# A convolution and ELU feed-forward kernel: four 64x64 array tiles for both matmuls, and the clamp of the exponential on GpSimd

## The chip, the cores and the metric

One core of one Trainium2 chip. Times are microseconds of device time (us). Unless a run says otherwise they are medians of timed runs; several experiments were run once ("one look"), and their state is then called unknown. Engines are named as in the profile: PE is TensorE, PEld its weight loads, DVE VectorE, ACT ScalarE, POOL GpSimd, SP SyncE, which here only issues DMAs.

## The reference

```python
# x (8, 4096, 192) float32, weight (8, 7), w_in (192, 2048), w_out (2048, 192)
w = softmax(weight)                       # per head, over 7 taps
attn[b, s, h*24+g] = sum_k w[h, k] * x[b, s-6+k, h*24+g]     # causal convolution
h = attn.reshape(32768, 192) @ w_in
g = where(h > 0, h, exp(min(h, 0)) - 1)   # ELU
out = g @ w_out                           # (32768, 192) float32
```

Two matmuls of 32768 x 192 x 2048, with an ELU on 32768 x 2048 values between them.

## The kernel before

Tokens go in 64 groups of 512. The convolution of a group is 40 small matmuls in four 32-column tiles of the array. Its 192 channels land in 2 x 128 partitions, 24 used of every 32, and w_in is padded to the same rows, so the first matmul takes two K steps of 128. A free row carries a bias of 1, so PSUM holds h+1.

```python
# PE, one chunk of 128 hidden units x 512 tokens: K = 2 x 128 with padding
pe.matmul(dst, wpadA[:, P*cc:P*(cc+1)], attnT[:, s, 0, :], start=True,  stop=False)
pe.matmul(dst, wpadB[:, P*cc:P*(cc+1)], attnT[:, s, 1, :], start=False, stop=True)
...
# ACT: E = exp((h+1) - 1), a bias tensor of -1
a.activation(E[:, C % NE, :], hps[...], ACT.Exp, bias=negone[:, 0:1], scale=1.0)
...
# DVE: max(min(E, 1), h+1) = ELU + 1, one instruction
v.scalar_tensor_tensor(out=gT[...], in0=E[...], scalar=1.0, in1=hps[...],
                       op0=ALU.min, op1=ALU.max)
...
# DVE: the output, minus the column sums of w_out, which takes the 1 away again
v.tensor_tensor(osb[...], ops_slot[CC % 2], negcs[:], ALU.add)
```

GpSimd only issues the loads of x and of the weights (float32 to narrower types on the way) and sets up constants.

## Time and profile before

| | before |
|---|---|
| time | 884.62 us (884.52 to 884.67) |
| PE, DVE, ACT, POOL busy | 95%, 83%, 80%, 11% of 882.3 us |
| one group of 512 tokens | 13.38 us, so 26.76 us per 1024 tokens |
| first matmul 128x512, start to start | 0.216 us |
| second matmul 128x192, start to start | 82.5 ns |

The first line below is the page's busy times by engine, with the share of the span and the number of instructions. The second is the chain that ended last, by engine: the last instruction followed back, step by step, to what released each one. The others are the page's groups: line, engine, operation, tiles, shapes, count; then busy us and mean ns of one; then the idle time before them and what ended most of it.

```profile
PE 833.8 (95%) x8594; PEld 561.6 (64%) x8722; DVE 730.6 (83%) x1300; ACT 709.1 (80%) x1160; POOL 98.9 (11%) x170
...
PE 80%; DVE 11%; ACT 6%; issue 2%
...
L456 DVE SCALAR_TENSOR_TENSOR gT<-E,hps 128x512 f16<-128x512 f32 x1024 | 652.2, 684 | 139.2 <-ACT E L424 136.7
L424 ACT ACTIVATE E<-hps,negone 128x512 f32<-128x512 f32 x1024 | 641.7, 689 | 121.5 <-PE hps L385 121.5
L340 PE MATMUL ops<-w_outq,gT 128*128 128x192 f16 x4096 | 421.2, 246 | 10.0 <-DVE gT L456 1.0
L385 PE MATMUL hps<-attnT,wpadB 128*128 128x512 bf16 x1022 | 388.1, 380 | 13.2 <-issue 9.8
```

PE is both the busiest engine and most of the chain. A matmul's recorded length overlaps the next one's, so its pace is read from the chain in order of time (start us, us, what): 0.22 for each first matmul, 0.66 for eight second ones.

```profile
403.28 0.22 PE hps L378
403.50 0.22 PE hps L385
...
404.14 0.66 PE ops L340 x8
```

One more line: the output DMAs on SP, with the least, median and greatest ns that one issue holds SP.

```profile
L473 SPq DMA_DIRECT2D out_dram<-osb x8: 332/332/333, 395.9 to 419.5; - x8
```

### The profile page before, as it was taken

To read this page: it belongs to the slowest core of one execution; us is meant where nothing else is said; L and a number is where in the kernel's file an instruction comes from. 1 tells how busy PE (TensorE), PEld (TensorE's weight loads), DVE (VectorE), ACT (ScalarE), POOL (GpSimd) and SP (SyncE) were. 2 spreads that over 40 slices of the span, in tenths; PEclk is the share of its full clock that TensorE was granted. 3 is DMA by queue.
4 is the path that set the end of the run, shared out by engine and by line. 5 is a ranking of instruction groups with operands and counts; after the bars stand their busy time and mean duration, and the time that the engine had idled before them with its cause. 6 is when DMAs were issued, how large, how long until landed. Compare 5 with 4: busy or idle time off the path is not lost.

```text
span 882.3 us, 21974 instructions
## 1 busy us (share of the span) xinstructions
PE 833.8 (95%) x8594; PEld 561.6 (64%) x8722; DVE 730.6 (83%) x1300; ACT 709.1 (80%) x1160; POOL 98.9 (11%) x170
## 2 busy tenths in 40 slices
PE   0899999999999999999999999999999999999998
PEld 0466666666666666666666666666666666666666
DVE  6788888888888888888888888888888888888886
ACT  2888888888888888888888888888888888888884
POOL 6101101001001011011011011011011011011000
DMA  7233233233233233232233232232232232232311
GB/s 93 34 50 55 41 54 55 39 56 50 44 55 51 45 55 51 43 55 49 46 51 53 46 51 50 47 52 47 48 55 46 48 56 45 50 55 41 54 33 42
DMA packets 82586, 43.89 MB, mean 50 GB/s; under 512 B 49523, under 2 KB 82291, under 8 KB 82483
## 3 DMA queue, kind: packets, MB, share of 16 engines
q0 software_dynamic: 45616, 17.30, 18.5%
q1 hardware_dynamic: 36866, 25.18, 9.2%
q8 instruction: 69, 1.13, 0.5%
q14 instruction: 35, 0.28, 0.1%
HBM read 34.57 MB, written 25.17 MB: 68 GB/s over the span
## 4 chain that ended last, share of the span: by engine, by line
PE 80%; DVE 11%; ACT 6%; issue 2%
PE ops L340 35%; PE hps L385 22%; PE hps L378 20%; DVE gT L456 10%; ACT E L424 5%; PE cps L300 4%; DVE Ttmp L267 1%; DVE Tm L270 0%; PE ops L357 0%; ACT L280 0%; DVE Tm L264 0%; ACT attnT L412 0%; ACT wpadB L282 0%; ACT wpadA L281 0%; ACT attnT L413 0%
## 5 line engine op out<-in xcount | busy, mean ns | idle before, releaser
L456 DVE SCALAR_TENSOR_TENSOR gT<-E,hps 128x512 f16<-128x512 f32 x1024 | 652.2, 684 | 139.2 <-ACT E L424 136.7
L424 ACT ACTIVATE E<-hps,negone 128x512 f32<-128x512 f32 x1024 | 641.7, 689 | 121.5 <-PE hps L385 121.5
L340 PEld LDWEIGHTS ops<-w_outq,gT 128*128 128x128 f16 x4096 | 348.2, 98 | 145.0 <-DVE gT L456 40.7
L340 PE MATMUL ops<-w_outq,gT 128*128 128x192 f16 x4096 | 421.2, 246 | 10.0 <-DVE gT L456 1.0
L385 PE MATMUL hps<-attnT,wpadB 128*128 128x512 bf16 x1022 | 388.1, 380 | 13.2 <-issue 9.8
L378 PE MATMUL hps<-attnT,wpadA 128*128 128x512 bf16 x898 | 341.9, 381 | 3.4 <-DVE gT L456 2.0
L378 PEld LDWEIGHTS hps<-attnT,wpadA 128*128 128x128 bf16 x1024 | 100.0, 98 | 82.0 <-DVE gT L456 15.6
L385 PEld LDWEIGHTS hps<-attnT,wpadB 128*128 128x128 bf16 x1024 | 100.4, 98 | 61.0 <-issue 0.8
L198 POOL DMA_DIRECT2D xg<-in_x_dram x64 | 48.1, 752 | 647.2 <-PE cps L300 621.2
L440 DVE TENSOR_TENSOR osb<-ops,negcs 128x192 f32<-128x192 f32 x256 | 89.9, 351 | 4.2 <-PE ops L340 4.2
L412 ACT ACTIVATE attnT<-cps 128x512 bf16<-128x512 f32 x64 | 38.2, 597 | 42.1 <-PE cps L300 42.1
L300 PE MATMUL cps<-Tm,xg 128*24 128x122 bf16 (+1 forms) x2560 | 41.8, 210 | 16.3 <-DVE Tm L270 16.3
L300 PEld LDWEIGHTS cps<-Tm,xg 128*24 128x24 bf16 x2560 | 33.2, 92 | 26.6 <-DVE Tm L270 16.4
L413 ACT ACTIVATE attnT<-cps 128x512 bf16<-128x512 f32 x64 | 37.8, 591 | 0.0
L200 POOL DMA_DIRECT2D xg<-in_x_dram x64 | 34.8, 544 | 0.0
L182 POOL MEMSET xg<- 6x192 bf16 x8 | 2.0, 248 | 82.5 <-PE cps L300 82.5
L267 DVE TENSOR_TENSOR Ttmp<-shift,wprb 128x976 bf16<-128x976 bf16 x6 | 7.1, 1176 | 0.2
L185 POOL DMA_DIRECT2D xg<-in_x_dram x8 | 4.5, 561 | 0.0
L270 DVE TENSOR_TENSOR Tm<-Tm,Ttmp 128x976 bf16<-128x976 bf16 x6 | 4.0, 667 | 0.2
L316 PE MATMUL ops<-wrow,onesF 1*128 1x56 f32 x2 | 0.6, 422 | 3.0 <-POOL onesF L157 3.0
L236 DVE TENSOR_REDUCE wmx<-ops 128x8 f32<-128x56 f32 x1 | 0.2, 217 | 3.7 <-PE ops L316 3.7
L316 PEld LDWEIGHTS ops<-wrow,onesF 1*128 1x128 f32 x2 | 0.5, 308 | 3.0 <-issue 3.0
(31 smaller groups left out, 22.3 us busy)
## 6 DMA issues: line engine op xcount, KB each, us to landing
out_dram<-osb SPq DMA_DIRECT2D x256, 96.0 KB, 1.6
xg<-in_x_dram POOLq DMA_DIRECT2D x56, 192.0 KB, 3.6
xg<-in_x_dram POOLq DMA_DIRECT2D x64, 48.0 KB, 3.6
xg<-in_x_dram POOLq DMA_DIRECT2D x8, 144.0 KB, 3.6
w_outq<-in_moe_w_out_dram POOLq DMA_DIRECT2D x1, 768.0 KB, 9.4
wpadA<-in_moe_w_in_dram POOLq DMA_DIRECT2D x4, 96.0 KB, 3.8
wpadB<-in_moe_w_in_dram POOLq DMA_DIRECT2D x4, 96.0 KB, 4.8
xg<-in_x_dram POOLq DMA_DIRECT2D x8, 45.8 KB, 2.3
```

Source lines behind the costliest of these rows:

```text
L198: g.dma_start(xg[:, s, w0:NWIN_FULL, :], src).then_inc(s_xin[s], 16)
L200: g.dma_start(xg[:, s, 4, :], x_flat[t0 + LASTW_ROW0 : t0 + GS, :]).then_inc(s_xin[s], 16)
L267: v.tensor_tensor(Ttmp[:, :, :], sd, wd, ALU.mult).then_inc(s_dset)
L300: ins = pe.matmul(cps[SLOT * q : SLOT * q + CH_PER_HEAD, col0 + ocol : col0 + ocol + ncol], xg[:, s, wdw, CH_PER_HEAD * hq : CH_PER_HEAD * ...
L340: ins = pe.matmul(bank, gT[:, slot, c, P * j : P * (j + 1)], w_outq[:, c, :], start=(c == 0), stop=(c == NCH - 1),)
L378: pe.matmul(dst, wpadA[:, P * cc : P * (cc + 1)], attnT[:, s, 0, :], start=True, stop=False,)
L385: pe.matmul(dst, wpadB[:, P * cc : P * (cc + 1)], attnT[:, s, 1, :], start=False, stop=True,).then_inc(s_mm1)
L412: a.activation(attnT[:, slot, 0, :], cps[:, 0:GS], ACT.Copy).then_inc(s_attn)
L413: a.activation(attnT[:, slot, 1, :], cps[:, GS : 2 * GS], ACT.Copy).then_inc(s_attn)
L424: a.activation(E[:, C % NE, :], hps[:, (C // 2) % NHTB, (C % 2) * GS : (C % 2) * GS + GS], ACT.Exp, bias=negone[:, 0:1], scale=1.0,).then_ ...
L440: v.tensor_tensor(osb[:, CC % 4, :], ops_slot[CC % 2], negcs[:], ALU.add).then_inc(s_oev)
L456: v.scalar_tensor_tensor(out=gT[:, G % 2, c, :], in0=E[:, C % NE, :], scalar=1.0, in1=hps[:, (C // 2) % NHTB, (C % 2) * GS : (C % 2) * GS ...
```

## The change

The intent is to take work off PE. 192 channels are exactly three K steps of 64, so in 64x64 tiles, four at once, the padding goes. That leaves no bias row, so PSUM holds h itself, and ELU becomes max(min(E, 1) - 1, h): the min and the subtraction go to the idle GpSimd, and VectorE keeps one maximum, over 1024 elements at once. Work goes in 32 supers of 1024 tokens, 16 pairs of hidden blocks each. The output matmuls ("rounds") of a super run three pairs behind the next super's. The convolution still writes 24 channels of every 32 partitions, so 20 SBUF-to-SBUF DMAs per super pack them into 64-row blocks, twice. Pairs and convolutions take turns in three PSUM buffers ("slots"): a slot is free for the next once VectorE, or for a convolution ACT, has read it.

```diff
+HALF_STEPS = (10, 9, 9, 9, 9, 9, 9)     # output rounds per pair
+CONV_AT = (2, 10)                       # pairs after which the next super's convolutions run
...
+                for u in range(2):                       # GpSimd
+                    W(s_exp, 2 * n + u + 1)
+                    g.tensor_scalar(out=E[:, n % NE, u, :], in0=E[:, n % NE, u, :],
+                        scalar1=1.0, scalar2=1.0, op0=ALU.min, op1=ALU.subtract,
+                    ).then_inc(s_clp)
...
-                    a.activation(E[...], hps[...], ACT.Exp, bias=negone[:, 0:1], scale=1.0)
+                        a.activation(E[:, n % NE, u, :], H[:, k, GS*u:GS*(u+1)], ACT.Exp)
...
-                    v.scalar_tensor_tensor(... op0=ALU.min, op1=ALU.max)
-                v.tensor_tensor(osb[...], ops_slot[...], negcs[:], ALU.add)
+                v.tensor_tensor(gT[... 1024], E[... 1024], H[:, slot, :], ALU.max)
...
+                    for j in range(3):                   # PE, first matmul
+                        for r in range(2):
+                            for c in range(2):
+                                pe.matmul(H[HP*c:HP*(c+1), k % 3, GS*r:GS*(r+1)],
+                                    w_in[HP*r:HP*(r+1), j, ...], att[HP*r:HP*(r+1), s % 2, j, c, :],
+                                    start=(j == 0), stop=(j == 2), tile_position=(HP*r, HP*c))
...
+                    for (hb, sl, r0, nr, j, d0) in MOVES:   # SP: 10 moves, two copies each
+                        for r in range(2):
+                            sy.dma_start(att[HP*r+d0 : HP*r+d0+nr, s % 2, j, :, :],
+                                csb[SLOT*sl+r0 : SLOT*sl+r0+nr, s % 2, hb, :, :]).then_inc(s_att, 16)
```

(Shortened, with cuts marked. GpSimd issues the x loads of a later super before its clamp of pair 8.)

## The prediction

> **What bounds the kernel now.** TensorE. In the page's first part PE is busy 95% of 882.3 us, DVE 83%, ACT 80%, POOL 11%; the chain that ended last is 80% PE. In the timeline a 512-token group takes 13.38 us (26.76 per 1024 tokens): 32 first matmuls 0.216 us apart (6.9), 64 second matmuls 82.5 ns apart (5.3), 40 convolution matmuls in 0.6, the rest short waits for exp and DVE. 64 groups are 856 us; head 22, tail about 8.
>
> **What the change removes and adds, per 1024 tokens (estimates from those durations).**
> - First matmul: K is 3x64 instead of 2x128 padded, so 16 pairs x 3 x 0.216 = 10.4 us instead of 13.8, if four 64x64 tiles stream together. The convolution's four column tiles do: 40 matmuls in 0.6 us.
> - Second matmul: same streaming, 128 rounds x 82.5 ns = 10.6 us, but four 64-column weight loads a round. The trace spaces its 24-column loads about 10 ns apart; if loads go one at a time, 64 columns are 27 ns and a round 107 ns, 13.7 us.
> - Convolution and switches about 2 us. PE sum 23 to 26 us.
> - ACT: exp without bias tensor should step by 0.50 us like the copies (0.58 now): 16 + evacuations 3.5 = 19.5.
> - DVE: one 128x1024 maximum, (1024+145)/0.96 = 1.22 us x 16 = 19.5; its 0.35 us output additions go.
> - POOL: 32 clamps. The Trainium skill ("GPSIMD Engine Reference", section 3.1) gives 1.03 cycles an element at 1.2 GHz for short bodies, about 0.55 us for 512; the affine select here ran nearer 1.5 ns an element, 0.85 us. So 18 to 27 us plus about 1.5 us of x issues.
> - PSUM: three slots shared by all; a slot's cycle is 0.8 + 1.1 + 0.65 + 1.25 + semaphores, about 4 us, 1.33 us a pair.
>
> **New critical path: the attention rearrangement.** After the convolution at pair 10, 20 SBUF-to-SBUF DMAs go out on SP before pair 0 of the next super may start. An SP issue takes 332 ns in the trace, and the skill ("Perfetto Trace Analysis", lifecycle of a hardware-DGE DMA) says the sequencer is free only at the profiled end: 6.6 us, plus about 1.6 to landing, plus convolution and evacuation, about 11 us from pair 10's first matmul. Only six steps of 1.4 us cover it. So PE stalls about 3 us per super, and the period is about 11.5 + ten steps (15) = 26.5 us, about what it was. Head grows to about 31 us (the same DMAs), tail to about 14 (a super's second matmuls).
>
> **Prediction.** 32 x 26.5 + about 40 = 890 us; range 800 to 985. Faster by over 2%: 0.33; within 2%: 0.22; slower: 0.45. The 3.4 us saved per 1024 tokens in the first matmul is mostly given back at the rearrangement and in the pipeline through four engines.
>
> **What would show it.** PE busy in steady stretches falls below 90%; the waits view shows first matmuls of pair 0 waiting 2 to 4 us for the att DMA, 31 times; SP issues of 0.33 us back to back, 20 in a row; first matmul rounds 0.216 us; second rounds 82 or 107 ns; exp 0.60 us long, 0.50 apart; clamps 0.55 or 0.85; DVE 1.22.
>
> **What would make it wrong.** Faster (about 800): SP issues overlap or the stall is hidden, leaving the 23 us PE sum. Slower (950 to 1000): weight loads serialise, or a clamp takes 0.85 us, making POOL the bound at 29 us per super.

## The result, and the profile after

2040.85 us (2040.48 to 2041.67, four runs) against 884.59 for the kernel before on the same chip: 2.307 times as long, 95% interval 2.304 to 2.311. A ratio here is the mean time of one kernel's fast runs over that of the other's of the same rounds, so not quite the ratio of the medians. The result is correct. The predicted range ended at 985 us.

The same parts of the page after the change:

```profile
PE 1057.4 (52%) x25088; PEld 692.6 (34%) x25088; DVE 640.8 (31%) x531; ACT 670.8 (33%) x1156; POOL 1991.8 (98%) x1120
...
POOL 97%; PE 1%; DVE 1%; SPq 1%; DMA 0%; ACT 0%; issue 0%; POOLq 0%
...
L237 POOL TENSOR_SCALAR E<-E 128x512 f32<-128x512 f32 x1024 | 1930.5, 1912 | 26.9 <-ACT E L284 26.4
L338 DVE TENSOR_TENSOR gT<-E,H 128x1024 f16<-128x1024 f32 x512 | 625.4, 1221 | 1377.0 <-POOL E L237 1377.0
L395 PE MATMUL H<-att,w_in 64*64 64x512 bf16 x6144 | 556.4, 478 | 729.5 <-DVE gT L338 682.7
L284 ACT ACTIVATE E<-H 128x512 f32<-128x512 f32 x1024 | 555.8, 595 | 1099.4 <-PE H L395 1099.4
```

One engine is busy 98% and is 97% of the chain, and each other engine waits for it in turn: VectorE for the clamp, TensorE for VectorE to free PSUM, ACT for TensorE. The clamp takes 1.91 us where the prediction had 0.55 to 0.85. The chain between two x loads holds 32 clamps in 60.33 us, 1.885 us each; with the two x issues (0.92 and 0.55 us) a super is 61.8 us, 32 of them 1978 us, and the first clamp starts at 39.6 and 19.7 us follow the last.

The timeline (start us, us, engine, line, operation, tiles, count, idle before in brackets) shows the rest of the design at the pace that was hoped for, whenever GpSimd lets it:

```profile
1013.34 7.56 POOL L237 TENSOR_SCALAR E<-E 128x512 f32<-128x512 f32 x4
...
1014.67 0.84 PE L395 MATMUL H<-att,w_in 64*64 64x512 bf16 x12 [0.76 <-DVE gT L338]
...
1015.35 0.91 PE L415 MATMUL ops<-w_out,gT 64*64 64x192 f16 x36
...
1016.09 0.82 PE L395 MATMUL H<-att,w_in 64*64 64x512 bf16 x12
...
1016.96 1.08 ACT L284 ACTIVATE E<-H 128x512 f32<-128x512 f32 x2 [0.30 <-PE H L395]
1017.16 1.22 DVE L338 TENSOR_TENSOR gT<-E,H 128x1024 f16<-128x1024 f32 x1 [2.54 <-POOL E L237]
```

From one first matmul to the next, with nine output rounds between, PE needs 1016.09 - 1014.67 = 1.42 us. Four clamps, two pairs, take 7.56. PE's granted clock is lower too, a mean of 0.74 over the run (1.00 before). That does not set the time: PE is 1% of the chain, and its first matmuls waited 407 times, 683 us in all, for VectorE to free a slot.

The last lines to compare are those of the DMAs on SP. One rearranging issue holds SP for 714 ns in the median, not 332:

```profile
L444 SPq DMA_DIRECT2D att<-csb x640: 535/714/1622, 21.2 to 1949.7; - x160
```

In the trace the 24-row moves take 714 to 770 ns, the 8-row ones 645, the 16-row ones 535 to 590; the first 20 together 14.6 us.

### The profile page after: what moved, and what is told of

Read it like the earlier page. It is cut to its first block, busy times and chain, and to the rows that moved or that the text cites. A ratio compares the mean times of both kernels' runs of the same rounds, so it can differ in the third digit from the quotient of the medians.

```text
span 2038.9 us, 54519 instructions
## 1 busy us (share of the span) xinstructions
PE 1057.4 (52%) x25088; PEld 692.6 (34%) x25088; DVE 640.8 (31%) x531; ACT 670.8 (33%) x1156; POOL 1991.8 (98%) x1120
## 4 chain that ended last, share of the span: by engine, by line
POOL 97%; PE 1%; DVE 1%; SPq 1%; DMA 0%; ACT 0%; issue 0%; POOLq 0%
POOL E L237 95%; POOL xg L201 1%; POOL xg L202 1%; SPq L444 1%; PE ops L415 1%; DVE Ttmp L323 0%; DVE Tm L327 0%; POOL xg L192 0%; DMA wq<-in_weight_dram 0%; DMA att<-csb 0%; ACT csb L273 0%; POOLq L105 0%; ACT osb L260 0%; PE H L395 0%; POOL xg L191 0%
## 5 line engine op out<-in xcount | busy, mean ns | idle before, releaser
L237 POOL TENSOR_SCALAR E<-E 128x512 f32<-128x512 f32 x1024 | 1930.5, 1912 | 26.9 <-ACT E L284 26.4
L338 DVE TENSOR_TENSOR gT<-E,H 128x1024 f16<-128x1024 f32 x512 | 625.4, 1221 | 1377.0 <-POOL E L237 1377.0
L395 PE MATMUL H<-att,w_in 64*64 64x512 bf16 x6144 | 556.4, 478 | 729.5 <-DVE gT L338 682.7
L284 ACT ACTIVATE E<-H 128x512 f32<-128x512 f32 x1024 | 555.8, 595 | 1099.4 <-PE H L395 1099.4
L415 PE MATMUL ops<-w_out,gT 64*64 64x192 f16 x16384 | 530.1, 285 | 7.5 <-DVE gT L338 6.1
L415 PEld LDWEIGHTS ops<-w_out,gT 64*64 64x64 f16 x16384 | 476.7, 130 | 138.6 <-issue 77.1
L395 PEld LDWEIGHTS H<-att,w_in 64*64 64x64 bf16 x6144 | 163.1, 123 | 925.5 <-DVE gT L338 753.1
L373 PE MATMUL H<-Tm,xg 128*24 128x122 bf16 (+3 forms) x2560 | 66.3, 284 | 240.4 <-DVE gT L338 222.3
L373 PEld LDWEIGHTS H<-Tm,xg 128*24 128x24 bf16 x2560 | 55.1, 129 | 278.0 <-DVE gT L338 154.2
L273 ACT ACTIVATE csb<-H 128x1024 bf16<-128x1024 f32 x64 | 65.4, 1023 | 234.5 <-PE H L373 234.5
```

Source lines behind the costliest of these rows:

```text
L237: g.tensor_scalar(out=E[:, n % NE, u, :], in0=E[:, n % NE, u, :], scalar1=1.0, scalar2=1.0, op0=ALU.min, op1=ALU.subtract,).then_inc(s_clp)
L273: a.activation(csb[:, s % 2, :, g, :], H[:, slot_of_conv[m] % 3, :].rearrange("p (b t) -> p b t", b=2), ACT.Copy,).then_inc(s_ce)
L284: a.activation(E[:, n % NE, u, :], H[:, k, GS * u : GS * (u + 1)], ACT.Exp).then_inc(s_exp)
L338: v.tensor_tensor(gT[:, s % NG3, 2 * q : 2 * q + 2, :].rearrange("p f t -> p (f t)"), E[:, n % NE, :, :].rearrange("p u t -> p (u t)"), H[ ...
L373: ins = pe.matmul(H[SLOT * q : SLOT * q + CPH, k % 3, GS * hb + o : GS * hb + o + nc_], xg[:, s % NXB, w, CPH * h : CPH * (h + 1)], Tm[:, ...
L395: ins = pe.matmul(H[HP * c : HP * (c + 1), k % 3, GS * r : GS * (r + 1)], w_in[HP * r : HP * (r + 1), j, HP * f : HP * (f + 1)], att[HP * ...
```

## The experiments

My theory after the result (A): the clamp costs 1.9 us by its nature and sets the time alone; below it lies the wait for the rearranging DMAs, larger than predicted. Rivals: VectorE's reading of the same tile, or the hand-over between engines, slows the clamp; or something else in the new structure is slow and the clamp only shows it. "Before" ran beside each at 884.2 to 884.5 us.

| run | what | us | result |
|---|---|---|---|
| e1_bench | before, with GpSimd measurements in its idle time | 883.97 (one look) | right |
| e2_noclamp | changed, no clamp | 1200.23 (one look) | Its output is wrong, which doesn't matter for the time. |
| e3_noclamp_early | e2, convolutions at pairs 1 and 2 | 854.55 (one look) | Its output is wrong, which doesn't matter for the time. |
| e4_early | changed, convolutions at pairs 1 and 2 | 2064.65 (one look) | right |
| e5_fma | changed, multiply and add on GpSimd | 1265.45 (one look) | right |
| e6_fma_early | e5, convolutions at pairs 1 and 2 | 903.33, ratio 1.022 (1.020 to 1.023) | right |
| e7_fma_early0 | e5, convolutions at pairs 0 and 1 | 905.74, ratio 1.024 (1.023 to 1.026) | right |
| e8_split | e2, half of the rearranging DMAs on GpSimd's queue | 1041.86 (one look) | Its output is wrong, which doesn't matter for the time. |
| e9_noload | e6 without x loads after the third super | 869.49 (one look) | Its output is wrong, which doesn't matter for the time. |
| e10_halves | e6, VectorE in halves | 871.70 (one look) | right |
| e11_best | e10, x loads spread, shorter head | 852.97, ratio 0.963 (0.961 to 0.966) | right |
| e12_dveclamp | changed, clamp on VectorE, convolutions at pairs 1 and 2 | 1051.35 (one look) | right |

### The clamp by itself

```diff
             for G in range(2, NG):
                 x_dmas(G)
+                if G - 2 < 3 * len(kinds):
+                    kinds[(G - 2) % len(kinds)]()    # one of 20 GpSimd instructions on scratch tiles
```

> The kernel before, with one unused GpSimd instruction on scratch tiles placed after each pair of x loads, 20 kinds, three of each; its result stays right and its time should stay within 1% of 884 us, since POOL was 11% busy. It measures the disputed cost by itself, with no clamp in the loop. Theory A (the clamp is slow by its own nature): min and subtract on 128x512 float32 takes about 1.9 us here too, as in the changed kernel. Theory B (it is slowed by the VectorE maximum reading the same tile, or by the pace of the loop): it takes 0.55 to 0.9 us here. Within A: if the cost is per operation, min alone or subtract alone takes about half, and a tensor copy about 0.55; if it is per byte, float16 takes about half; if it is fixed per instruction, 128 columns take nearly as long as 512; if writing in place hurts, the same into another tile is faster.

The timeline of GpSimd in this run, a line for each kind. In order they are: min and subtract into another tile; min alone; subtract alone; multiply and add; then min and subtract again, on 128 columns, on 1024, and on float16; a plain copy; and add and add.

```profile
30.56 1.94 POOL L251 TENSOR_SCALAR bb<-ba 128x512 f32<-128x512 f32 x1
44.00 1.51 POOL L249 TENSOR_SCALAR bb<-ba 128x512 f32<-128x512 f32 x1
57.32 1.52 POOL L249 TENSOR_SCALAR bb<-ba 128x512 f32<-128x512 f32 x1
70.99 0.63 POOL L251 TENSOR_SCALAR bb<-ba 128x512 f32<-128x512 f32 x1
...
97.94 0.66 POOL L251 TENSOR_SCALAR bb<-ba 128x128 f32<-128x128 f32 x1
110.60 3.64 POOL L251 TENSOR_SCALAR bb<-ba 128x1024 f32<-128x1024 f32 x1
123.92 1.93 POOL L251 TENSOR_SCALAR hb<-ha 128x512 f16<-128x512 f16 x1
...
163.83 0.62 POOL L266 COPY bb<-ba 128x512 f32<-128x512 f32 x1
...
257.53 1.96 POOL L251 TENSOR_SCALAR bb<-ba 128x512 f32<-128x512 f32 x1
```

Theory A holds and B falls: the same instruction takes 1.94 us in a kernel that never waits for it. Between 512 and 1024 columns it grows by 1.70 us, 3.3 ns a column, so the cost is mostly per column, not per instruction. Type makes no difference, nor does writing in place (1.97), nor half the partitions (1.96). The surprise is the operation. Min alone or subtract alone costs 1.5 us, more than the half that a cost per operation would give; add and add take 1.96, but multiply and add 0.63, as little as a copy. Why this one pair is fast the runs do not show, and the multiplier was 1 in every run, so that another one is as fast was not tried.

### Without the clamp

```diff
-                for u in range(2):
-                    W(s_exp, 2 * n + u + 1)
-                    g.tensor_scalar(... op0=ALU.min, op1=ALU.subtract).then_inc(s_clp)
...
-                W(s_clp, 2 * n + 2)      # VectorE
+                W(s_exp, 2 * n + 2)
```

> The changed kernel without the GpSimd clamp; VectorE takes the maximum with the raw exp, so the result is wrong on purpose. Theory A (the clamp alone sets 2041 us, and the attention rearrangement is the next bound): pair 10 to the end of the convolution evacuation about 3 to 4 us, 20 SP issues that now measure 14.6 us in the trace of the changed kernel, 2 us to landing, then ten steps of 1.42 us and a convolution, 34 to 35 us per 1024 tokens, so 1120 to 1180 us. Theory B (next bound is TensorE, the rearrangement being hidden): 24 us per 1024 tokens, 800 to 830 us. Theory C (something else in the changed kernel is slow and the clamp only showed it): over 1500 us.

1200 us: 841 us less than the changed kernel, nearest to theory A though 20 us above its range, and still far above TensorE's own pace. Waits (total us, times, longest) and timeline of this run:

```profile
PE H L385 <- DMA att<-csb: 322.7, 32, 17.7
```

```profile
598.96 10.73 SPq L434 DMA_DIRECT2D att<-csb  x15
...
600.07 0.98 PE L405 MATMUL ops<-w_out,gT 64*64 64x192 f16 x36
...
611.09 1.50 PE L385 MATMUL H<-att,w_in 64*64 64x512 bf16 x12 [10.03 <-DMA att<-csb]
```

The first matmul of each super stands still for about 10 us while SP is still issuing moves.

### The convolutions earlier, without and with the clamp

```diff
-CONV_AT = (2, 10)
+CONV_AT = (1, 2)
```

> The run without the clamp, and both convolutions of the next super at pairs 1 and 2 instead of 2 and 10 (one constant), so that the 20 rearranging DMAs have 13 steps to land instead of five. Result still wrong on purpose. Theory A: the wait of pair 0 for the rearrangement goes, TensorE bounds at 24 to 25 us per 1024 tokens, 810 to 860 us. If the rearrangement was not what bound the run without the clamp, this changes nothing, within 2%.

> The changed kernel with only the convolutions moved to pairs 1 and 2, the clamp still on GpSimd. Theory A (GpSimd is busy 98% and sets the time alone): 2041 us within 1%. Rival (the late rearrangement costs the changed kernel time too, as the prediction had it, about 3 us or more per super): 1900 to 1950 us.

Without the clamp this one constant is worth 346 us (1200 to 854.55): the 20 issues now have 13 pairs to finish in. The wait left over, and the busy times by engine of e2_noclamp and of this run:

```profile
PE H L385 <- DMA att<-csb: 44.0, 20, 17.2
...
PE 809.3 (68%) x25088; PEld 585.6 (49%) x25088; DVE 638.5 (53%) x531; ACT 650.3 (54%) x1156; POOL 61.2 (5%) x96
...
PE 745.7 (87%) x25088; PEld 559.9 (66%) x25088; DVE 631.9 (74%) x531; ACT 645.7 (76%) x1156; POOL 59.1 (7%) x96
```

The stall costs more than its length. The wait shrinks by 279 us (322.7 to 44.0), and the same matmuls are recorded as busy for 64 us less, together about the 346. In e2_noclamp, 12 first matmuls just after a stall take 1.50 us in the chain, and 0.84 a few pairs later; the mean granted clock is 0.856, against 0.994 in this run.

With the slow clamp it buys nothing. The run came out 24 us slower than the changed kernel, where 1% (20 us) had been allowed. What GpSimd waited for before its clamps, and the first matmul's weight loads for the rearrangement, in the changed kernel; then GpSimd's wait in e4_early:

```profile
POOL E L237 <- ACT E L284: 26.4, 1, 26.4
PEld H L395 <- DMA att<-csb: 71.6, 30, 3.4
...
POOL E L237 <- ACT E L284: 49.2, 32, 26.4
```

The bound engine is now starved about 0.7 us per super, 31 times. By the code, two convolutions close together take two of the three PSUM slots, which would explain it. So the wait for the rearrangement, which the prediction made the bound, cost the changed kernel as good as nothing; it was hidden behind the clamp.

### The same ELU in other operations

For every h, E - 1 >= h, so ELU is also min(max(h, 0), E - 1). The part without h can then be multiply by 1, add -1.

```diff
-                        scalar2=1.0, op0=ALU.min, op1=ALU.subtract,
+                        scalar2=-1.0, op0=ALU.mult, op1=ALU.add,
...
-                v.tensor_tensor(gT, E, H, ALU.max)
+                v.scalar_tensor_tensor(out=gT, in0=H, scalar=0.0, in1=E, op0=ALU.max, op1=ALU.min)
```

> The changed kernel with the same ELU in other operations: GpSimd makes E-1 as multiply by 1, add -1 (0.63 us for 128x512 in the bench run, where min and subtract took 1.94), and VectorE makes min(max(h,0), E-1), one scalar_tensor_tensor in place of one maximum. The result should be right. Convolutions stay at pairs 2 and 10. Theory A (the pair of operations, not GpSimd as such, cost the time; then the rearranging DMAs bind as without the clamp): clamps of 0.6 to 0.65 us, and 1200 to 1260 us, like the run without the clamp (1200). Theory B (GpSimd in the loop keeps it slow, by contention or by hand-over): clamps over 1 us and more than 1400 us.

> The run with multiply and add, and the convolutions at pairs 1 and 2. Right result. Theory A: both causes undone; TensorE at 1.39 us a pair in the run without the clamp, plus a PSUM slot's cycle lengthened by one 0.63 us clamp to about 4.0 us (1.33 a pair): 850 to 890 us, so within 2% of the kernel before or up to 4% faster. If the longer slot cycle binds: over 900 us.

> As the run before it, with the convolutions one pair sooner, at pairs 0 and 1, since without the clamp and with pairs 1 and 2 pair 0 still waited for the rearranging DMA 20 times, 44 us in all. Theory: 1 us per 1024 tokens off, 20 to 40 us faster than with pairs 1 and 2. If VectorE, ACT or the PSUM slots bound it by then: same within 1%.

The group of the GpSimd instruction, with the convolutions at pairs 2 and 10:

```profile
L237 POOL TENSOR_SCALAR E<-E 128x512 f32<-128x512 f32 x1024 | 612.4, 621 | 571.1 <-ACT E L284 570.6
```

621 ns in the loop, as in the bench, and VectorE's instruction takes 1225 ns, as the maximum did. The time falls from 2041 to 1265 us with a right result, 5 us above theory A's range: GpSimd as such was not the trouble, the pair of operations was. With the convolutions at pairs 1 and 2 it is 903 us, 13 us above theory A's range, where a PSUM slot cycle that binds had been expected, and 2.2% slower than before. Moving them one pair further gave nothing (expected: 20 to 40 us, or the same within 1% if something else bound by then); in the 903 us run the wait for the DMAs was already down to 17.9 us in two waits, nearly all of it the first super's.

What is left shows in the timeline of the 903 us run:

```profile
505.94 0.59 POOL L192 DMA_DIRECT2D xg<-in_x_dram  x1
...
506.52 0.99 POOL L201 DMA_DIRECT2D xg<-in_x_dram  x1
...
507.50 0.59 POOL L202 DMA_DIRECT2D xg<-in_x_dram  x1
...
509.36 3.52 DVE L338 SCALAR_TENSOR_TENSOR gT<-H,E 128x1024 f16<-128x1024 f32 x3 [2.30 <-POOL E L237]
510.64 0.84 PE L397 MATMUL H<-att,w_in 64*64 64x512 bf16 x12 [2.60 <-DVE gT L338]
```

x loads stand in GpSimd's queue between clamps, and VectorE and TensorE stop behind them. Between such stops TensorE runs at its own pace in the critical chain:

```profile
501.10 0.74 PE ops L417 x36
501.84 0.65 PE H L397 x12
```

### Issue time or transfer

```diff
-                        for r in range(2):
+                        for r in range(1):               # SP: one copy
                             sy.dma_start(att[HP*r + d0 ...
+                for (hb, sl, r0, nr, j, d0) in MOVES:    # GpSimd queue: the other copy
+                    g.dma_start(att[HP + d0 ...]).then_inc(s_att2, 16)
```

(Shortened. With no clamp on GpSimd, its queue holds only x loads and these moves, a super's x load before them.)

> The run without the clamp (result wrong on purpose, convolutions at pairs 2 and 10), with ten of the 20 rearranging DMAs of each super issued from the idle GpSimd queue instead of SP. The same bytes move between the same tiles. Theory A (the issue time on SP, 0.54 to 0.76 us each, is what is waited for): SP's 14.6 us becomes 7.3 with GpSimd's 6 to 7 beside it, 7 us less per super, so 960 to 1000 us against 1200. Theory B (the transfers or their landing are what is waited for, the issues only queue behind them): 1150 to 1200 us.

```profile
PE H L400 <- DMA att<-csb: 181.7, 32, 16.9
```

158 us less for the same bytes, 5 us per super: outside both ranges, between them and nearer A. TensorE's wait per super goes from 10.1 us (322.7/32) to 5.7 (181.7/32). The share of the chain in the transfers themselves rises from 6% of 1198 us to 14% of 1040, from about 2 to 4.6 us per super, so part of what the second queue saves comes back as a longer landing.

### The rest of the loss, and a version that beats both

```diff
 # e9:  -                if i == 8 and s + NXB < NS: load_x(s + NXB)
 #      and the semaphore counts that waited for those loads
 # e10: VectorE's instruction on 512 columns, twice, each after its own clamp
 # e11: e10, and
-                if i == 8 and s + NXB < NS:
-                    load_x(s + NXB)
+                if i in (5, 8, 12) and s + NXB < NS:
+                    load_x(s + NXB, ((5, 8, 12).index(i),))
 #      and for the first super, one copy of each move on GpSimd's queue, as in e8
```

> The run with multiply, add and convolutions at pairs 1 and 2 (903 us), without the x loads of supers 3 and later, so that old x is used again; the result is wrong on purpose. In that run's trace GpSimd issues two or three x loads at pair 8, 1.5 to 2.4 us, and VectorE, TensorE then wait 2.3 to 2.6 us. Theory A (those issues, in the queue between the clamps, cost the time that is left): 1.5 to 2.5 us per super less, 830 to 860 us. Theory B (the longer PSUM slot cycle alone costs it): 890 to 905 us.

> The 903 us run with VectorE's 128x1024 instruction cut in two of 128x512, each started by its own clamp, so that the first half of VectorE's work overlaps the second clamp and the slot's cycle is about 0.5 us shorter. VectorE's work rises from 1.22 to about 1.28 us a pair. Theory: with slack in the slot cycle, part of the stalls at the x loads and convolutions is absorbed: 865 to 890 us. If the slot cycle doesn't matter: 900 to 910.

> An attempt at a version that beats both: the run with VectorE in halves, and x loads spread over pairs 5, 8 and 12 instead of all at 8, and half of the first super's rearranging DMAs from the then idle GpSimd queue (head about 7 us shorter). Right result. Theory: 835 to 865 us, 2 to 5% faster than the kernel before. If neither matters: as the run with halves.

(The diff is shortened.) Without the x loads the time falls by 34 us, about 1 us per super: the loads do cost time, but less than the 43 us at least that theory A had. VectorE in halves, with all loads in place, gains about as much (871.7 us, 1.4% under the kernel before in one look): the second clamp overlaps the first half, and TensorE's wait for VectorE to free a slot falls from 95.4 to 59.2 us. So loads and slot cycle both had a share. Together with spread loads and a shorter head, the kernel is right and 3.7% faster than before:

```profile
PE 746.7 (88%) x25088; PEld 554.3 (65%) x25088; DVE 661.3 (78%) x1043; ACT 652.0 (77%) x1156; POOL 677.3 (80%) x1130
```

How the last 19 us divide between spread loads and head was not tried separately.

### The clamp on VectorE

```diff
+                v.tensor_scalar(out=e2, in0=e2, scalar1=1.0, scalar2=1.0,     # 128x1024 float32
+                                op0=ALU.min, op1=ALU.subtract).then_inc(s_clp)
+                W(s_clp, n + 1)
```

> The changed kernel with its own min and subtract moved from GpSimd to VectorE, as one 128x1024 float32 instruction before the maximum, and convolutions at pairs 1 and 2. Right result. Theory: VectorE becomes the bound with 1.22 plus 0.6 to 0.7 us a pair, 30 us per 1024 tokens, 960 to 1040 us: far better than on GpSimd in this form, but slower than the kernel before. If it runs at one element a cycle (1.2 us): 1250 us.

```profile
L327 DVE TENSOR_SCALAR E<-E 128x1024 f32<-128x1024 f32 x512 | 352.3, 688 | 55.0 <-ACT E L274 55.0
```

The same min and subtract take 688 ns for 1024 columns on VectorE and 3640 on GpSimd. VectorE is then busy 91%, and 1051 us is 11 us above the range: a far better place for these operations (e4_early, with the same convolutions, takes 2065), but no gain over the kernel before.

## Why the prediction was wrong

- **The step that failed: "POOL: 32 clamps", 18 to 27 us per 1024 tokens.** It was 60.3 us, and POOL, not the rearrangement, set the period: 61.8 us per super against the 26.5 predicted. The prediction took a rate from the Trainium skill ("GPSIMD Engine Reference", section 3.1) and set a ceiling of 0.85 us from the affine select, another instruction. e1_bench shows 1.94 us for these very operations with no loop around them. Its last paragraph did name a slow clamp as what would make it wrong, but at less than half the size.
- **What followed from it.** With POOL at 61.8 us per super no other term could bind: e4_early shows that the wait for the DMAs, the prediction's new critical path, cost nothing there. Its sign did appear in the changed kernel, near the predicted 2 to 4 us, 31 times: the weight loads waited 71.6 us in 30 waits. But GpSimd waited only once, before its first clamp. That agreement was luck: a wait that is there need not be one that costs.
- **The rearrangement: right mechanism, wrong size.** Twenty issues "in 6.6 us" took 14.6; the 332 ns came from 128-partition output DMAs, and moves of 24 or 8 rows take 714 and 645. Once the clamp is gone it is the bound, 1200 us, with a 10 us stall where the prediction had 3. One constant removes nearly all of it. So even with a clamp of 0.63 us the predicted 890 would have been missed: e5_fma is 1265.
- **What held.** Four 64x64 tiles stream together: in the critical chain of e6_fma_early, 12 first matmuls take 0.65 us (three rounds of 0.216) and 36 output matmuls 0.74 (nine rounds of 82 ns), so the fear of serial weight loads was groundless. Two exps take 1.08 us, the maximum 1.22. "ScalarE: Activation LUTs" of the skill, on what an ACTIVATE costs, agrees: it takes about 93 ns off for a bias that is not a tensor, and the exp went from 689 to 595 ns. The first matmul's saving of 3.4 us per 1024 tokens is real, 109 us in all, but no version turned more than part of it into time: e11_best is 31.5 us faster than the kernel before.
- **The reported chances** gave 0.45 to slower. The sign was therefore the likeliest of the three, but mainly for another reason, the rearrangement; the clamp that decided it stood there only as a case of 950 to 1000 us. That the sign came out right was mostly luck.

## What to carry to other kernels

Before work goes to an engine that is idle, time the exact instruction there, with its operations and width; a page's rate and another instruction's duration gave 0.55 and 0.85 us where 1.91 was measured, and a bench in the idle time of a running kernel cost under 0.1% of it. When one engine hides everything else, take it away with a wrong result: that showed the next bound (1200 us) and the one after it (854 us) in two runs. And an algebraic identity that changes the operations, here min and subtract to multiply and add, can be worth more than a move to another engine (903 us against 1051, with the same convolutions).

## What the Trainium skill lacked or had wrong

- "GPSIMD Engine Reference", section 3.1, has 1.03 cycles an element for bodies of at most two operations, and section 4.1, which advises VectorE for elementwise work, calls one-input work on GpSimd roughly line-rate. Here min and subtract grow by 3.3 ns a column, 4.0 cycles at the page's 1.2 GHz, and min or subtract alone takes 1.51 and 1.52 us for 512. Only multiply and add (0.63 us) and a copy (0.62 us) come near the page's figure (0.44 us, an estimate from it without dispatch). The page has higher costs for other kinds of loop body, but not that min, subtract or two additions cost two to three times as much as multiply and add.
- "Perfetto Trace Analysis", section "DMA Instruction — HWDGE", says rightly that the sequencer is held to the profiled end: 20 issues of 0.54 to 0.77 us follow one another with about 0.04 us between them. No page gives an issue time by shape: 332 ns for 128 rows, 714 for 24, 645 for 8 and 535 to 590 for 16 (the 128-row DMAs write to DRAM, the others to SBUF, so rows are not the only difference). "DMA: Bandwidth & Descriptors", on why a DMA increments its semaphore by 16, says that such a DMA is split over the largest divisor up to 16 of its rows, by that rule 12, 8 and 16 engines here for 24, 8 and 16 rows; that this is why the times differ is not shown.
- "TensorEngine Tiling (Array Packing)", section Restrictions, says that column tiling disables fast weight load. The page gives no size for the loss, and none is seen here: a round of four 64x64 loads and four 192-column matmuls still takes 82 ns, as one 128x128 load and matmul did before (82.5).

